# The first batch of a one-core attention and MLP kernel in a form of its own: doubled fp32r products, row sums by TensorE, bf16 transposes of W_tok, dummy products and another load order

## The chip, the core and the metric

The kernel runs on one core of a Trainium2 chip. The metric is the time of one execution on the device in microseconds (us); less is better. A profile is one such execution; its span is 1.8 to 2.1 us below the time of the same run. TensorE (PE) multiplies, ScalarE (ACT), VectorE (DVE) and GpSimd (POOL) do the rest, SyncE (SP) issues transfers. With one core there is no second die to compare with, so runs are labelled slow or fast by their times.

## The reference

Eight batches; per batch eight heads of 576 rows and 64 columns. Attention without softmax, an RMS norm over the 64 columns, then a token-mixing and a channel-mixing layer.

```python
kv  = einsum('bhsd,bhse->bhde', k, v)
out = einsum('bhsd,bhde->bhse', q, kv)
x   = out / sqrt(mean(out*out, -1) + 1e-6) * g_norm     # then to [b, 576, 512]
a1  = alpha1 * x + beta1
u   = x + lam * einsum('ts,bsd->btd', w_tok, a1)        # "tok"
a2  = alpha2 * u + beta2
y   = u + lam * (maximum(a2 @ w_ch1, 0) @ w_ch2)        # "ch1", "ch2"
```

The biases beta1 and beta2 are folded into spare rows, lam into W2 and the row sums of W_tok.

## The kernel before

The kernel describes each operation with its engine (or several to choose from), an assumed cost, what it reads and writes, and a priority. A list scheduler in the program, run when the kernel is built, turns this into one fixed order per engine. On the chip the orders are kept, with semaphores in between: an instruction that waits holds up what stands behind it on its engine (the stall of 3.30 us shown below is one).

Some terms. A main is the transfer of the first 512 rows of q, k or v of a batch (1 MB), a tail that of the last 64 (128 KB). A staging slot is a buffer in which a main or a block of weights lands. A cast or rounding copies it from there in the type that the products take; fp32r is the type of the rounded fp32 operands of kv, the q transposes and the attention output. An eviction copies the result of a product out of TensorE's accumulators. The result of a dummy product is not used.

```python
def load(b, pri):                      # batch 0: v on ScalarE's queue, the rest on SyncE's
    aq = "AQ" if b == 0 else "SP"
    load_main("k", k, b, "SP", pri)
    load_main("v", v, b, aq, pri)
    load_tail("k", kvft, k, b, 0, "SP", pri)       # rows 512 to 575
    load_tail("v", kvft, v, b, 64, aq, pri)
    load_main("q", q, b, "SP", pri)
    ...
# norm, per chunk of 128 rows
P.op({"ACT": act_us(512)}, ... ACT.Square ...)
P.op({"DVE": dve_us(512)}, ... tensor_reduce(out=small[rows, s4], in_=sq[rows, s2], ...) ...)
P.op({"ACT": 0.3}, ... ACT.Sqrt ...)
P.op({"DVE": 0.2}, ... reciprocal ...)
P.op({"DVE": dve_us(512)}, ... yn = product * scale ...)
...
# W_tok: 25 fp32 transposes, five evictions on ScalarE, then column sums by TensorE
P.op({"PE": 0.12}, lambda e, _, ...: e.transpose(t..., wrow(tc, sc), ident[0:rr, 0:rr]), ...)
```

Lines of the profile name products by what they write and read: `ps<-vr,kr` is kv, `ps<-identr,qr` the q transposes, `ps<-kvc,qt` or `ps<-kr,qt` the attention output, `ps<-rt,wt` tok, `ps<-a2t,w` ch1, `ps<-w,ht` ch2.

## Time and profile before

| kernel before | us |
|---|---|
| median of 3 runs (lowest, highest) | 385.44 (384.83, 387.29) |
| span of the profiled run (386.89 us) | 385.1 |
| first ch1 product starts | 52.49 |
| from there to the end of the last product | 327.31 |
| closing add and store | 5.31 |
| TensorE at half clock | 13.8 to 41.1, and by the pace of the dummies (one every 0.43 us) before 7.0, where no clock is recorded |

The start of the first ch1 product splits the kernel into the preparation of the first batch and TensorE's main work.

### The profile page before, as it was taken

Reading aid. Unit: us, or ns where it says so; the run is one execution under the profiler, and the core shown is the slowest. Engines: PE = TensorE matmul, PEld = TensorE weight load, DVE = VectorE, ACT = ScalarE, POOL = GpSimd, SP = SyncE. Lnnn points to the kernel's source line nnn. Section 1 sums busy time; section 2 is a strip of 40 time slices with the busy share of each in tenths; the row PEclk is TensorE's granted clock in tenths of the full one; section 3 lists DMA queues with packets and bytes.
Section 4 is the critical chain, followed back from the end, with each engine's and each line's share of the span. In section 5 each row is a group of like instructions: output and inputs, shape, how many; then the busy total and the mean of one; then the engine's idle time right before and its main releaser. Section 6 shows DMA issues by size and latency. Waiting matters only on the chain.

```text
span 385.1 us, 5526 instructions
## 1 busy us (share of the span) xinstructions
PE 371.8 (97%) x2243; PEld 228.4 (59%) x2243; DVE 224.6 (58%) x370; ACT 179.1 (47%) x309; POOL 81.2 (21%) x61
## 2 busy tenths in 40 slices
PE   5799999999999999999999999999999999999994
PEld 2496456557977656455875566456765544547641
DVE  6317689999696848665945398336815582520021
ACT  1346665756773727622662246423752165206400
POOL 2007242542034305101410034003400141000000
PEclk9755899999999999999999999999999999999998
DMA  8994799997994564402000111002000120010022
GB/s 236 305 380 146 210 384 327 303 277 238 329 306 140 155 203 136 139 2 83 29 0 2 54 56 28 0 29 75 9 2 27 54 56 0 25 59 27 2 82 54
DMA packets 47377, 47.83 MB, mean 124 GB/s; under 512 B 13869, under 2 KB 38453, under 8 KB 47224
## 3 DMA queue, kind: packets, MB, share of 16 engines
q1 hardware_dynamic: 45760, 46.29, 38.6%
q10 hardware_dynamic: 1592, 1.19, 1.1%
q8 instruction: 17, 0.28, 0.3%
q14 instruction: 8, 0.07, 0.1%
HBM read 38.04 MB, written 9.44 MB: 123 GB/s over the span
## 4 chain that ended last, share of the span: by engine, by line
PE 86%; DVE 8%; DMA 3%; issue 0%; ACTq 0%; ACT 0%
PE ps L700 30%; PE ps L720 30%; PE ps L634 11%; PE ps L595 3%; PE ps L539 3%; DMA st<-in_v_dram 3%; PE ps L557 3%; DVE w L904 2%; PE ps L661 2%; PE ps L849 2%; PE ps L788 1%; DVE qr L397 1%; DVE yn L610 1%; DVE small L602 1%; PE ps L867 1%; DVE vr L397 1%
## 5 line engine op out<-in xcount | busy, mean ns | idle before, releaser
L700 PE MATMUL ps<-a2t,w 128*128 128x320 bf16 (+1 forms) x768 | 141.7, 329 | 0.0
L720 PE MATMUL ps<-w,ht 128*128 128x512 bf16 x576 | 138.4, 382 | 0.0
L700 PEld LDWEIGHTS ps<-a2t,w 128*128 128x128 bf16 x768 | 73.5, 98 | 41.5
L685 ACT ACTIVATE ht<-ps 128x640 bf16<-128x640 f32 (+1 forms) x110 | 71.8, 653 | 51.2 <-PE ps L700 50.7
L720 PEld LDWEIGHTS ps<-w,ht 128*128 128x128 bf16 x576 | 54.6, 98 | 58.4
L620 POOL TENSOR_TENSOR xm<-yn,g_bc 128x512 f32<-128x512 f32 x22 | 37.0, 1680 | 167.4 <-DVE yn L610 166.7
L728 DVE TENSOR_TENSOR xm<-ps,xm 128x512 f32<-128x512 f32 x32 | 22.0, 689 | 57.7 <-PE ps L720 57.4
L600 ACT ACTIVATE sq<-ps 128x512 f32<-128x512 f32 (+1 forms) x40 | 23.7, 593 | 48.9 <-PE ps L595 48.6
L634 PE MATMUL ps<-rt,wt 128*128 128x512 bf16 x160 | 42.7, 381 | 0.0
L641 DVE TENSOR_TENSOR xm<-ps,xm 128x512 f32<-128x512 f32 x32 | 21.9, 689 | 34.9 <-PE ps L634 34.7
L539 PE MATMUL ps<-vr,kr 128*128 128x128 f32 x128 | 37.0, 387 | 2.0 <-DVE vr L397 1.9
L557 PE MATMUL ps<-identr,qr 128*128 128x128 f32 x128 | 37.0, 394 | 0.0
L595 PE MATMUL ps<-kvc,qt 128*128 128x128 f32 x128 | 36.5, 388 | 0.0
L602 DVE TENSOR_REDUCE small<-sq 128x8 f32<-128x512 f32 (+1 forms) x40 | 26.9, 677 | 16.0 <-ACT sq L600 15.6
L539 PEld LDWEIGHTS ps<-vr,kr 128*128 128x128 f32 x128 | 25.9, 217 | 3.5 <-DVE vr L397 3.0
L610 DVE TENSOR_TENSOR yn<-ps,small 128x512 f32<-128x512 f32 (+1 forms) x40 | 27.3, 685 | 0.6
L595 PEld LDWEIGHTS ps<-kvc,qt 128*128 128x128 f32 x128 | 25.9, 216 | 2.2 <-DVE qt L397 0.2
L615 POOL TENSOR_TENSOR rt<-yn,ge 128x512 bf16<-128x512 f32 x13 | 18.4, 1414 | 39.6 <-DVE yn L610 39.2
L557 PEld LDWEIGHTS ps<-identr,qr 128*128 128x128 f32 x128 | 26.1, 218 | 0.9 <-issue 0.3
L634 PEld LDWEIGHTS ps<-rt,wt 128*128 128x128 bf16 x160 | 15.4, 98 | 17.2 <-DVE xm L641 0.3
L396 ACT ACTIVATE qt<-ps 128x512 fp32r<-128x512 f32 x27 | 16.1, 597 | 16.1 <-PE ps L557 15.9
L788 PE MATMUL ps<-identb 128*128 128x512 bf16 x47 | 14.7, 454 | 4.2 <-DVE identb L771 4.2
(93 smaller groups left out, 346.8 us busy)
## 6 DMA issues: line engine op xcount, KB each, us to landing
st<-in_k_dram SPq DMA_DIRECT2D x8, 1024.0 KB, 8.5
st<-in_q_dram SPq DMA_DIRECT2D x8, 1024.0 KB, 7.3
st<-in_moe_w_ch_dram SPq DMA_DIRECT2D x8, 1024.0 KB, 11.7
out_dram<-xm SPq DMA_DIRECT2D x32, 256.0 KB, 2.3
st<-in_v_dram SPq DMA_DIRECT2D x7, 1024.0 KB, 6.3
ht<-in_moe_w_tok_dram SPq DMA_DIRECT2D x1, 1152.0 KB, 13.5
kvft<-in_k_dram SPq DMA_DIRECT2D x8, 128.0 KB, 4.8
qft<-in_q_dram SPq DMA_DIRECT2D x8, 128.0 KB, 7.5
```

The source lines that it names most:

```text
L539: return e.matmul(t.flat()[:, 128 * pr:128 * pr + 128], a, m, start=(c == 0), stop=(c == 4))
L557: return e.matmul(t.flat()[:, 128 * pr:128 * pr + 128], a, identr[:], start=True, stop=True)
L595: return e.matmul(t.flat()[:, 128 * pr:128 * pr + 128], a, kvc[:, b % 2, pr, :], start=True, stop=True)
L600: P.op({"ACT": act_us(512)}, lambda e, _: e.activation(flat(sq[rows, s2]), t.flat(rows), ACT.Square), r=[t], w=[("sq", s2)], pri=p)
L602: P.op({"DVE": dve_us(512)}, lambda e, _: e.tensor_reduce(out=small[rows, s4], in_=sq[rows, s2], axis=AX.X, op=ALU.add), r=[("sq", s2)], w ...
L610: P.op({"DVE": dve_us(512)}, lambda e, _: e.tensor_tensor(out=hview(yn[rows, s3, :]), in0=hview(t.flat(rows)), in1=small[rows, s4][:, :, N ...
L620: lambda e, _: e.tensor_tensor(out=hview(x), in0=hview(yn[rows, s3, :]), in1=g_bc[rows, None, :].to_broadcast([nr, NH, DH]), op=ALU.mult),
L634: return e.matmul(t.flat(), wt[:, sc, col:col + 128], rt[:, sc, :] if sc < 4 else rtt[:], start=(sc == 0), stop=(sc == 4))
L685: return e.activation(dst, src(), ACT.Relu)
L700: return e.matmul(o, w1[:, dj, 128 * fj:128 * fj + 128], m, start=(dj == 0), stop=(dj == 3))
L720: P.op({"PE": 0.216}, lambda e, _: e.matmul(t.flat(), ht[:, fj, 128 * c:128 * c + 128], w2[:, fj, :], start=(fj == 0), stop=(fj == 15)), r ...
L728: P.op({"DVE": dve_us(512)}, lambda e, _: e.tensor_tensor(out=x, in0=t.flat(), in1=x, op=ALU.add), r=[t] + keys, w=keys, pri=p - 2)
```

## The change

Its intent is to shorten those 52 us: q, k, v load first; the products that cannot be wide are doubled to 256 columns so that TensorE counts as busy; dummy products fill TensorE's idle time from 1 us on; the sums of squares of batch 0 go to TensorE (transposed products, squared, multiplied by a block of ones); W_tok is transposed in bf16; a sixth staging slot lets loads run further ahead. The cost table of the scheduler changes too, so every order in the kernel is new. Core of the diff, cuts marked:

```diff
-        st = sb("st", [128, 5, 2048], F32)
+        st = sb("st", [128, NS, 2048], F32)                  # NS = 6
+        hot = sb("hot", [128, 128], BF16)                    # operand of the dummies
+        blk = sb("blk", [128, 2], F32)                       # ones, per head
...
             aq = "AQ" if b == 0 else "SP"
+            load_main("q", q, b, "SP", pri)
             load_main("k", k, b, "SP", pri)
-            load_main("v", v, b, aq, pri)
-            load_tail("k", kvft, k, b, 0, "SP", pri)
+            load_main("v", v, b, "SP", pri, 2 if b == 0 else 1)
+            if b == 0:
+                load_tail("q", qft, q, 0, 0, aq, pri)
+            load_tail("k", kvft, k, b, 0, aq, pri)
             load_tail("v", kvft, v, b, 64, aq, pri)
...
+        def norm_first(pri):
+            def sums(pr, c):
+                P.op({"PE": 0.1}, lambda e, _: e.matmul(
+                    ts.flat()[:, 8 * c + 2 * pr:8 * c + 2 * pr + 2],
+                    sqt[:, pr, 128 * c:128 * c + 128], blk[:], start=True, stop=True), ...)
+            for pr in range(4):
+                ... # transposed product of 512 columns, Square on ScalarE into sqt (fp32)
+                for c in range(4):
+                    sums(pr, c)
+            ... # the last 64 rows likewise; one Sqrt and one reciprocal for all
...
+            for i in range(2):
+                P.op({"POOL": pool_us(1152, False)}, ...)     # W_tok to bf16 on GpSimd
...
-                P.op({"ACT": act_us(512)} if qn < 2 else {"ACT": ..., "DVE": ...}, ...)   # W1
+                P.op({"ACT": act_us(512)} if qn < 3 else {"ACT": ..., "DVE": ...}, ...)
-                P.op({"POOL": pool_us(1024), "DVE": dve_us(1024)}, ...)                   # W2
+                P.op({"POOL": pool_us(1024)} if hh else {"DVE": dve_us(1024)}, ...)
-        norm(0, -400)
+        norm_first(-400)
```

## The prediction

> **What bounds the kernel now.** I read the page's tenths, then the windows table, the chain that ended last in order of time, the groups by line, and last the matmul-by-matmul timeline of TensorE and the DMA issues. The page first:
>
> ```profile
> span 385.1 us, 5526 instructions
> ...
> PE   5799999999999999999999999999999999999994
> ...
> PEclk9755899999999999999999999999999999999998
> DMA  8994799997994564402000111002000120010022
> ```
>
> TensorE looks full everywhere, but its granted clock is low in the first five slices (48 us), and DMA pauses in slice 5. The windows table (columns: stretch and its length, then busy time of PE, PEld, DVE, ACT, POOL with counts, granted clock, DMA share, GB/s) separates the start:
>
> ```profile
> 0.00:13.60 13.60, 9.44 (x30) 3.53 (x30) 6.63 (x17) 3.51 (x7) 1.96 (x9) 1.00 0.91 260
> 13.60:15.50 1.90, 0.00 (x1) 0.00 (x0) 1.23 (x1) 1.55 (x3) 0.00 (x0) 0.56 1.26 243
> 15.50:41.00 25.50, 24.72 (x97) 18.97 (x97) 12.26 (x26) 11.84 (x24) 8.20 (x6) 0.50 0.71 247
> 41.00:52.50 11.50, 11.42 (x69) 5.61 (x69) 9.32 (x16) 7.75 (x14) 1.42 (x2) 0.99 1.02 316
> ```
>
> After 1.9 us in which TensorE had nothing to do, the whole first batch, 15.5 to 41 us, ran at half clock. The chain shows what the time was spent on (start, us, what):
>
> ```profile
> 2.97 11.26 DMA st<-in_v_dram
> 14.26 1.24 DVE vr L397
> ...
> 17.96 3.31 PE ps L539 x16
> ...
> 22.57 3.52 PE ps L557 x17
> ...
> 27.37 3.63 PE ps L595 x17
> 31.00 1.22 PE ps L849 x5
> ...
> 32.94 5.41 PE ps L849 x20
> 38.35 1.82 PE ps L867 x4
> ```
>
> It waits for v, rounds it, and then goes in single file through kv, the q transposes, the q·kv products (all fp32r with 128 columns), the fp32 transposes of W_tok (L849) and its column sums; tok follows at 44 us and the first ch1 matmul (L700) starts at 52.5 us, in the timeline. From there I compared start-to-start times: 216 ns for a bf16 matmul of 512 columns, 136 for 320, 56 for a transpose, and 74 for an fp32r matmul between bf16 ones (251 + 39 - 216). Summing the matmuls at these prices from 52.5 us to the last one at 379.8 gives 324 us of 327.3, so only 3.2 us are lost after the start, nearly all before 130 us. The last 5.3 us are the closing add and store. So the steady part is TensorE's work itself, and the change can win only in the first 52.5 us.
>
> **What the Trainium skill says.** "TensorE: Matmul & The Clock Gate", § What's actually happening: the array has half its clock until a free-running window of 3413 ns was busy, and loses it after an idle one. The trace agrees on the window: its clock changes come at 7.0, 13.8 and 41.1 us, and 41.1 - 13.8 is 8 x 3.41. It records no clock before 7.0, but dummies from 4.16 us start every 0.43 us, twice the 0.216 of later ones. It adds something: fp32r matmuls that keep TensorE "busy" for 20 us did not bring the clock back; the 512-column sums (L867) did. Same page, § LDWEIGHTS: columns / 1.2 ns, 107 ns for 128. The trace's back-to-back fp32r pairs start 213 ns apart at half clock (107 of load + 107 of streaming) and about 161 at full (107 + 54), so such loads are not hidden behind each other. "DMA: Bandwidth & Descriptors", § Issuing engines are not separate DMA queues: queues share the same 16 engines. It agrees: v, issued at 2.97 us on ScalarE's queue, landed at 14.2 after sharing with q, which landed at 13.2. "SBUF — State Buffer", § Who interferes with whom: VectorE copies in two-port mode and operations on two SBUF inputs block against GpSimd for a whole instruction. It agrees: the 128x512 cast of q takes 427 ns, but 2584 ns beside GpSimd's 128x1024 multiply.
>
> **The change, part by part.** I place the first ch1 matmul anew.
>
> Loads. Before, 1 MB each of k, q, v and the 64-row tails were in at 13 to 16 us, W_tok at 20.4, W1 at 22.8, 25.6, 28.3 and 32.1 (2.7 us per MB). The new order q, k, v with tails on the other queue carries 3.1 MB + 0.4 MB before W_tok. The bytes counted over time in the old trace pass 3.55 MB at about 13.5 us; so q lands near 6.5, k near 10, v (in two halves) near 12 and 13.5, W_tok near 18, W1 by 29. v itself gains under 1 us. But q's rounding and transposes (4 casts, 20 matmuls, 5 evictions of 0.6 us) now fit ahead of v.
>
> Products. After v: two casts side by side (0.42 on VectorE, 0.62 on ScalarE), 14.3 us; second half of kv, 10 matmuls of 256 columns at 0.117 (the kernel's assumption) to 0.214 (107 + 107), 16.2; small evictions, 16.9. Duplicating the columns costs streaming time; its point is that the array counts as busy, with the dummies, which now start near 1 us instead of 4.2. If the clock holds, dummies and products run at full rate.
>
> Norm. Before, each of five chunks had a square, reduce (0.68), sqrt (0.30), reciprocal (0.19) and multiply (0.69) in turn. Now ScalarE squares a transposed product for 5 x 0.6 us, two of them before v's second half, TensorE sums by 20 tiny fp32 matmuls (two 0.1 us loads each, some 0.25 us with streaming, 1 us of it after the last square), one sqrt, one reciprocal: scales ready near 21 us. Then VectorE makes five x (0.69) and three rt (0.69) while GpSimd makes two rt (1.41 each): 5.5 us, 26.5; with W_tok's evictions on the same engine and some blocking by GpSimd, 28.5.
>
> W_tok. GpSimd casts 2880 columns; at 0.74 us per 512, 4.2 us after 18, i.e. 22. 25 bf16 transposes at 0.056 to 0.11 us replace 25 fp32 ones that took 6.6 us; five evictions on two engines, 2 us; sums 1.3; two vector steps 0.65 + 0.82: 27. So it ends beside the norm chain, not after it.
>
> Tok and on. Four of five products per chunk can run ahead. After the last operand (28.5): one matmul, four adds of 0.69 in turn, a cast 0.63, transposes, a scaled eviction 0.77: 4.6 us, 33. In-order queues filled from an assumed timetable, not from events, usually cost some; I add 2.5 us. The first ch1 starts near 35.5 instead of 52.5: **17 us**.
>
> After it. TensorE's work is unchanged (four more fp32r matmuls for batch 1's own tail, 0.3 us). But batch 1 and W2 now come later relative to ch1: q1, k1, v1 follow W1 at about 32, 35 and 38 us, W2 at 41 to 49, scaled near 53, while the first ch2 (18 us after ch1 in the old trace: 71.0 - 52.5) wants it from 54. The sixth slot matters here: before, v of batch 1 sat 18 us behind a ScalarE cast that had to free its slot. VectorE was busy 41 of 44 us between 52 and 96 and takes on 2.5 us of rounding that used to precede ch1. I expect 4 us lost in place of 3.2. Sum: 385.4 - 17 + 0.3 + 0.8 = **369.5 us**.
>
> **Rivals.** (1) The gain shrinks to 8 to 10 us, 376: VectorE/GpSimd blocking or W2's scaling (2.4 us a half on GpSimd, 1.1 to 2.9 on VectorE) becomes the new limit after ch1. For it: VectorE's 95% there and a DMA that then must run without pause to about 60 us. Against it: TensorE has 5 us of batch 1's fp32r work to fill in with, and 20 MB, all that is needed through batch 2, is in by 60 us at 0.36 MB/us. (2) The clock stays low in spite of dummies because TensorE stands before an operand that comes late, and dummies behind it cannot run: the first batch's products and tok would then take about twice as long, some 4 us more, 373. For it: one gap of 1.9 us cost the clock for 27 us before. (3) Everything fits as the new timetable assumes: ch1 near 32.5, 366. Slower than before would need the stall after ch1 to grow by 17 us; I see nothing of that size.
>
> **Range and chances.** Start of ch1 between 31 and 41, losses after it of 2 to 8 us: 363 to 377. Over 2% faster means under 377.7; that needs 8 of the 17 us. Faster 0.94, within 2% 0.05, slower 0.01.
>
> **What would show it.** Right: first ch1 at 33 to 39 us, clock full from about 7 us through the first batch, bf16 transposes of W_tok under 3 us in all, DMA without the pause of slice 5, the same 216/136/74 ns after it and the same 5 us of tail. Wrong: half clock again between 15 and 40; VectorE instructions of 2 us and more while GpSimd casts W_tok; TensorE gaps between 40 and 80 us that end with W2 or a rounding of batch 1; or a different pace after 130 us, which I take as untouched.

## The result

The changed kernel took 397.32 us (median of 4 runs, 395.19 to 399.92), beside 385.66 for the kernel before (4 runs). The ratio is 1.03, 95% interval 1.0225 to 1.0375: about 3% slower. Ratios here are the mean time of one kernel's fast runs over the mean of the other's of the same rounds, so not quite the ratio of the medians quoted.

The page of the changed kernel (tenths in 40 slices of 9.9 us):

```profile
span 394.5 us, 5549 instructions
...
PE   8789988999979999899999999999999999999994
...
PEclk9865699999999999999999999999999999999999
DMA  8996599999864921821100011002000210020021
```

TensorE is busier in the first two slices than before, then the clock is low in slices 3 to 5. New dips of PE stand in slices 12 and 17, long after the start. Measured as before: ch1 begins at 56.73 us (before 52.49), from there to the last product 332.36 (before 327.31), tail 5.36. So of the 9.4 us that the span grew, 4.2 came before ch1 and 5.1 after it. (The medians differ by 11.7 us. The profiled run of the kernel before was a slow one, 386.89 us, and that of the changed kernel was below its median, 396.33.) The windows table of the changed kernel (stretch and length, then busy time of PE, PEld, DVE, ACT, POOL with counts, granted clock, DMA share, GB/s):

```profile
14.00:22.04 8.04, 4.74 (x23) 2.92 (x21) 2.15 (x6) 0.76 (x2) 4.30 (x4) 0.92 1.03 323
22.04:27.10 5.06, 5.06 (x12) 2.58 (x10) 1.80 (x6) 2.88 (x9) 0.00 (x0) 0.50 1.05 387
27.10:38.60 11.50, 11.50 (x57) 11.38 (x56) 1.39 (x2) 1.63 (x3) 0.00 (x0) 0.50 0.77 255
38.60:45.90 7.30, 7.05 (x37) 4.14 (x37) 4.16 (x7) 4.32 (x8) 2.55 (x2) 0.50 0.19 46
```

TensorE was idle for 3.3 of the 8.04 us of the first stretch. Then the clock was half for 24 us (22.0 to 45.9; it had been half from 11.8 to 15.2 as well), and for 11.5 of these (third row) TensorE was full while the three other engines did almost nothing. The transfers paused too: their share falls to 0.77 and 0.19, while SyncE's next load waited 16.1 us for ScalarE's rounding of W1 to free a staging slot. TensorE's timeline names the pieces (start, us, engine, line, product, count, and in brackets the idle time before it and what ended it):

```profile
21.45 0.76 PE L598 MATMUL ps<-vrt,krt 128*128 128x256 f32 x4 [3.30 <-DVE vrt L400]
...
27.13 1.87 PE L717 MATMUL ps<-blk,w 128*128 128x2 f32 x8
28.86 0.45 PE L732 MATMUL ps<-qtt,kvc 128*128 128x128 f32 x1
29.11 1.81 PE L717 MATMUL ps<-blk,w 128*128 128x2 f32 x8
```

Two things stand out. The stall of 3.30 us ends with the rounding of v's tail, vrt. And each eight of the sum products with the ones block take about 1.8 us; 40 of them are recorded where the program has 20, so each fp32 sum runs as two, some 0.21 us each at half clock. Lastly the tails among the DMA issues (KB, us from issue to landing):

```profile
qft<-in_q_dram ACTq DMA_DIRECT2D x1, 128.0 KB, 8.7
kvft<-in_k_dram ACTq DMA_DIRECT2D x1, 128.0 KB, 10.5
kvft<-in_v_dram ACTq DMA_DIRECT2D x1, 128.0 KB, 16.0
```

v's tail of 128 KB, issued at 4.66 us, landed at 20.69, after both parts of W_tok (18.71 and 19.38), which were issued later. The trace says how. Its packets by queue (1 is SyncE's, 10 ScalarE's), counted from its records:

```
window us   queue 1                          queue 10
14 to 16    82 packets, 722 KB (9216 B)      81 packets,  21 KB (256 B)
16 to 18   149 packets, 450 KB (2 to 9 KB)  148 packets,  37 KB (256 B)
```

The sizes in brackets are those of the packets that carry nearly all bytes. In these windows the two queues send packet for packet (from 10 to 14 us as well, 813 against 806), so the queue with 256-byte packets got a thirty-fifth of the other's bytes in the first window (21 against 722 KB) and a twelfth in the second. After 18 us the tail had fewer packets left than the other queue sent (88 against 173 up to 19.4 us).

### The profile page after: what moved, and what is told of

The parts are those of the page before. It is cut to its first block, busy times and chain, and to the rows that moved or that the text cites. A ratio compares the mean times of both kernels' runs of the same rounds, so it can differ in the third digit from the quotient of the medians.

```text
span 394.5 us, 5549 instructions
## 1 busy us (share of the span) xinstructions
PE 375.2 (95%) x2240; PEld 232.9 (59%) x2271; DVE 231.4 (59%) x383; ACT 173.8 (44%) x300; POOL 81.4 (21%) x61
## 3 DMA queue, kind: packets, MB, share of 16 engines
q1 hardware_dynamic: 45760, 47.08, 38.5%
## 4 chain that ended last, share of the span: by engine, by line
PE 84%; DVE 9%; DMA 4%; issue 1%; ACTq 1%; ACT 1%
PE ps L858 32%; PE ps L838 29%; PE ps L771 10%; DMA kvft<-in_v_dram 4%; PE ps L584 4%; PE ps L598 2%; PE ps L717 2%; PE ps L799 2%; DVE vr L400 1%; DVE yn L698 1%; DVE ht L824 1%; PE ps L996 1%; DVE small L686 1%; DVE kr L400 1%; PE ps L580 1%
## 5 line engine op out<-in xcount | busy, mean ns | idle before, releaser
L823 ACT ACTIVATE ht<-ps 128x512 bf16<-128x512 f32 (+1 forms) x111 | 72.0, 649 | 52.5 <-PE ps L838 52.0
L704 POOL TENSOR_TENSOR xm<-yn,g_bc 128x512 f32<-128x512 f32 x28 | 45.0, 1607 | 184.7 <-DVE yn L698 184.2
L684 ACT ACTIVATE sq<-ps 128x512 f32<-128x512 f32 (+1 forms) x35 | 20.7, 592 | 47.7 <-PE ps L584 47.4
L598 PE MATMUL ps<-vr,kr 128*128 128x128 f32 (+1 forms) x128 | 35.8, 373 | 2.9 <-DVE vr L400 2.9
L808 ACT ACTIVATE a2t<-ps,cols 128x512 bf16<-128x512 bf16 (+1 forms) x16 | 12.4, 826 | 47.6 <-PE ps L799 47.6
L584 PE MATMUL ps<-kvc,qt 128*128 128x128 f32 x112 | 33.0, 387 | 0.0
L584 PE MATMUL ps<-identr,qr 128*128 128x128 f32 x112 | 29.6, 362 | 0.0
L701 DVE TENSOR_TENSOR rt<-yn,ge 128x512 bf16<-128x512 f32 x28 | 26.7, 955 | 0.4
L771 PEld LDWEIGHTS ps<-rt,wt 128*128 128x128 bf16 x160 | 15.5, 98 | 17.6
L698 DVE TENSOR_TENSOR yn<-ps,small 128x512 f32<-128x512 f32 (+1 forms) x35 | 24.0, 685 | 0.5
L584 PEld LDWEIGHTS ps<-kvc,qt 128*128 128x128 f32 x112 | 22.3, 199 | 2.3
L584 PEld LDWEIGHTS ps<-identr,qr 128*128 128x128 f32 x112 | 21.2, 200 | 0.6
L399 ACT ACTIVATE qt<-ps 128x512 fp32r<-128x512 f32 x25 | 14.8, 595 | 7.0 <-PE ps L584 6.9
```

The costliest lines, as they stand in the source:

```text
L584: return e.matmul(t.flat()[:, 128 * pr:128 * pr + 128], a(), m(), start=start, stop=stop)
L598: return e.matmul(t.flat()[:, at:at + w], a, m, start=(c == 0), stop=(c == 4))
L698: P.op({"DVE": dve_us(512)}, lambda e, _: e.tensor_tensor(out=yn[rows, s3, :].rearrange("p (r h d) -> p r h d", r=4, h=2), in0=heads(t, b, ...
L701: P.op({"DVE": dve_us(512), "POOL": pool_us(512)}, lambda e, _: e.tensor_tensor(out=rto, in0=yn[rows, s3, :], in1=ge1[rows, :], op=ALU.mul ...
L704: P.op({"POOL": pool_us(512)}, lambda e, _: e.tensor_tensor(out=hview(x), in0=hview(yn[rows, s3, :]), in1=g_bc[rows, None, :].to_broadcast ...
L771: return e.matmul(t.flat(), wt[:, sc, col:col + 128], rt[:, sc, :] if sc < 4 else rtt[:], start=(sc == 0), stop=(sc == 4))
```

## The experiments

All kernels gave correct results. The first theory is that two faults add up: the late tail (stall, and with it the clock) and the fp32 sums. Its rivals are that either is enough, that the clock goes anyway, or that the new order as such is bad. In the second series one of seven runs of the kernel before took 758.73 us; it is not among the fast runs.

### Tails on SyncE's queue, orders otherwise the same (e1)

```diff
-        P.schedule()
+        P.schedule(); [setattr(o, "eng", "SP") for o in P.ops if o.kind == "L" and o.eng == "AQ"]
```

> The same program on every compute engine; only the three 64-row tails of batch 0 go out on SyncE's queue after v instead of on ScalarE's. Theory (late tail): v's tail lands by about 17 us instead of 20.7, the 3.3 us stall of TensorE before the vrt products goes under 0.5 us, the clock is not lost at 22.0 us, and the first ch1 matmul comes 8 to 12 us earlier than 56.7; time about 388. Rival (the small fp32 sums lose the clock by themselves): the stall goes, but the clock still falls in one of the next windows (25 to 29 us), the first ch1 comes 3 to 5 us earlier; time about 393.

Measured: 389.63 us median of four runs, 383.5 to 391.52. Three were labelled slow and one fast (383.5, mean granted clock 0.983 against 0.966 to 0.971), which here means that the clock was low for a shorter time, so I give no ratio. The profiled run is one of the slow ones (389.59). In it v's tail landed at 14.8 and the stall was gone; ch1 began at 48.34. But the clock fell all the same at 20.0 us and stayed at half until 37.1 (a line of TensorE's timeline, then one of the windows table):

```profile
16.03 0.74 PE L598 MATMUL ps<-vrt,krt 128*128 128x256 f32 x4 [0.29 <-DVE vrt L400]
...
20.00:37.10 17.10, 16.86 (x83) 14.00 (x83) 5.13 (x9) 5.95 (x11) 3.75 (x4) 0.50 0.95 321
```

The late tail explains the stall and, in this profile, 8.4 us of the start of ch1; the clock needs more than its absence.

### bf16 squares and ones, tails still late (e2)

```diff
-        blk = sb("blk", [128, 2], F32)
+        blk = sb("blk", [128, 2], BF16)
-        sqt = w2f[:, 0:2560].rearrange(...)
+        sqt = w2[:].rearrange("p j c -> p (j c)")[:, 0:2560].rearrange(...)
```

> The same order on every engine; squares and the block of ones are bf16, so each of the 20 sums is one matmul instead of two. Theory (sums mis-sized): the 40 sum matmuls take 8.4 us of TensorE in the current kernel; 20 at 0.11 us take 2.2, so the first ch1 comes about 6 us earlier even with the late tail; time about 391. If the sums lie beside other waits (W_tok's casts, ScalarE): under 2 us, 396.

Measured: 390.1 us (389.22 to 390.33), ratio 1.011 (1.0083 to 1.0137); ch1 at 48.96. TensorE's timeline of this run:

```profile
21.28 1.23 PE L598 MATMUL ps<-vrt,krt 128*128 128x256 f32 x4 [4.37 <-DVE vrt L400]
...
27.43 0.26 PE L717 MATMUL ps<-blk,w 128*128 128x2 bf16 x4
27.56 0.45 PE L732 MATMUL ps<-qtt,kvc 128*128 128x128 f32 x1
```

The stall is still there and longer, but each sum is one product now, and four of them let the next product start 0.13 us after the first. In all they lie between 27.4 and 31.4 in place of 27.1 and 38.5, also at half clock. So the sums, too, are worth 7 us by themselves.

### Both repairs (e3)

> Tails on SyncE's queue and bf16 sums together. If late tail and sums are the two causes, the clock stays full through the first batch and ch1 starts at 38 to 42 us, time 378 to 383, under before. If the clock is lost for another reason, ch1 at 46 to 50 and about 388.

Measured: 379.17 us (378.04 to 379.76), ratio 0.9827 (0.9799 to 0.9856). That is 18.1 us less than the changed kernel and better than the kernel before. TensorE's page row, clock row and timeline:

```profile
PE   8898999999799998999999999999999999999994
...
PEclk9999699999999999999999999999999999999999
```

```profile
16.05 0.74 PE L598 MATMUL ps<-vrt,krt 128*128 128x256 f32 x4 [0.38 <-DVE vrt L400]
...
19.46 0.25 PE L717 MATMUL ps<-blk,w 128*128 128x2 bf16 x4
19.58 0.31 PE L732 MATMUL ps<-qtt,kvc 128*128 128x128 f32 x1
...
20.51 1.17 PE L580 MATMUL ps<-kr,qt 128*128 128x256 f32 x8
...
27.60 4.49 PE L771 MATMUL ps<-rt,wt 128*128 128x512 bf16 x20
31.93 1.24 PE L771 MATMUL ps<-rtt,wt 128*128 128x512 bf16 x5
...
34.62 1.27 PE L584 MATMUL ps<-identr,qr 128*128 128x128 f32 x7 [1.24 <-DVE qr L400]
```

The clock was full from 4.2 to 38.4 us and ch1 began at 40.76. In the profiles ch1 moves from 56.7 to 48 or 49 with one repair and to 40.8 with both: about 8 us each, and together their sum. The clock is lost for one period of 6.8 us at 38.4.

### Filling the stall with more dummies (e4)

The tail stays late; the four dummies ahead of the vrt products are issued five times each.

```diff
-                ins = o.fn(eng, o.eng)
+                ins = [o.fn(eng, o.eng) for _ in range(self.times.get(o, 1))][-1]
... # self.times is 5 for those four dummies
```

> The late tail stays; the four dummies ahead of the vrt products are issued 20 times (4.3 us), so that TensorE is busy during the stall. Theory (the stall costs by the clock, not by its 3.3 us): the clock is not lost at 22.0 us; if the sums hold it, ch1 comes 6 to 10 us earlier, about 389. If the sums cannot hold it, it falls some 3.4 to 6.8 us later and ch1 comes under 3 us earlier, about 395.

Measured: 394.55 us (393.82 to 394.75), ratio 1.0226 (1.0199 to 1.0253). Its timeline:

```profile
16.16 4.49 PE L931 MATMUL ps<-hot 128*128 128x512 bf16 x20
20.93 0.74 PE L598 MATMUL ps<-vrt,krt 128*128 128x256 f32 x4 [0.28 <-DVE vrt L400]
...
24.34 1.48 PE L717 MATMUL ps<-blk,w 128*128 128x2 f32 x8
```

The stall is filled and the clock is kept past it, to 24.8 us; then it falls until 41.8. The fp32 sums had begun only 0.4 us before; the work of the window ahead of the fall is that of e1's (see the clock, below). ch1 began at 53.27, 3.5 us earlier, and the time fell by 2.8 us. So a filled stall alone is worth little: the clock was only saved to be lost 2.7 us later than in the changed kernel.

### GpSimd's halves of the W2 scaling given to VectorE (e5)

This looks at the 5.1 us after ch1. In the changed kernel GpSimd scales four halves of W2 between 56.4 and 66.8 us, and VectorE's two roundings of v (batch 1) at that time are slow. The rows are count and duration in ns (least, median, most), then first and last start, of the changed kernel:

```profile
L400 DVE CAST vr<-st x2: 2681/2758/2834, 56.6 to 59.2; 128x1024 fp32r<-128x1024 f32 x2
```

```profile
L1048 POOL TENSOR_TENSOR w<-st,lam_bc x4: 2346/2548/2692, 56.4 to 64.4; 128x1024 bf16<-128x1024 f32 x4
```

```diff
-        P.schedule()
+        P.schedule(); [setattr(o, "eng", "DVE") for o in P.ops if o.tag[:3] == "w2." and o.eng == "POOL"]
```

> The changed kernel with one thing moved: the four halves of W2 that GpSimd scales are given to VectorE, at the same place of the order; nothing else differs. Theory (GpSimd's 2.5 us multiplies block VectorE's two casts of batch 1's v, which take 5.4 us in place of 1.3, and TensorE waits 2.9 us for them after the first ch1): the two casts take 0.7 each, the waits of TensorE between 57 and 63 us fall from 2.9 to under 0.7 us; VectorE gains 4 x 1.1 us of work, which may give up to 2 us back later; time 393 to 396. Rival (v is late by its DMA): the waits stay, time 398 or more.

Measured: 393.06 us (389.96 to 394.78), ratio 1.0188 (1.0129 to 1.0247). The same row in this run:

```profile
L400 DVE CAST vr<-st x2: 673/674/674, 58.4 to 59.0; 128x1024 fp32r<-128x1024 f32 x2
```

The same roundings took a quarter of the time, TensorE's wait of 2.9 us for them was gone, and the part after ch1 fell from 332.36 to 329.17. In this profile ch1 began 1.5 us later (58.28; half clock from 12.5 to 50.0), so its span shows less of the gain (1.7 us) than the medians do (4.3).

### The norm as before, tails repaired (e6)

```diff
-            aq = "AQ" if b == 0 else "SP"
+            aq = "SP"
-        norm_first(-400)
+        norm(0, -400)
```

> Tails on SyncE's queue, and the first batch's norm per chunk as before (square, reduce, sqrt, reciprocal, multiply), without the sums by TensorE; everything is put in order anew. If the sums by TensorE are what made the first batch slow once the tails are in time, this is close to the kernel with bf16 sums or better: ch1 at 40 to 44 us, time 378 to 384. If the transposed sums are in principle better and only their fp32 form is wrong, this is 3 to 6 us slower than the bf16 sums: 382 to 386.

Measured: 389.45 us (385.68 to 391.27), ratio 1.0091 (1.0014 to 1.0167); ch1 at 47.99, with the clock lost three times before 53 us. That is outside both expected ranges. The edit goes in before the timetable is made, so the order changes too. Beside e3 (379.17) the kernel with row sums by TensorE in bf16 is some 10 us faster. How much of that is the norm and how much the new order and its clock was not separated. Nor does it say what the fp32 form gained: e1's runs lie on both sides of this one.

### A timetable made for later landings (e7)

Both repairs put in before the scheduler runs, a sum counted as 0.06 us, and transfers assumed to land 0.5 to 2 us later.

```diff
-                        o.end = dma_free + 2.0
+                        o.end = dma_free + (2.5 if dma_free < 15 else 4.0)
```

> Tails on SyncE's queue and bf16 sums, and the timetable that orders the instructions is told later landings (2.5 us after the transfer for the first loads, 4.0 for later ones, in place of 2.0) and 0.06 us per sum; everything is put in order anew. Theory (VectorE stands 1.9 us in order before the cast of batch 1's q, with the five adds of tok behind it, because the timetable has that load 2 us early): that idle time goes, the clock is not lost at 38 us, ch1 starts at 37 to 39 us in place of 40.8; time 374 to 377. Rival (such waits merely move): within 1.5 us of 379.

Measured: 381.66 us (380.95 to 382.15), ratio 0.99 (0.9875 to 0.9924). ch1 came earlier than in e3 (39.84), but the part after it was 335.14, with waits at new places. It lost 4 us there and gained 1 ahead, and lies outside both expected ranges.

### Both repairs, no dummies (e8)

> The kernel with tails on SyncE's queue and bf16 sums, its dummies dropped and nothing else changed. If the dummies make the clock of the first batch: half clock until about 25 us or later, ch1 3 to 8 us later than 40.8, time 382 to 387. If the products of 256 columns do it by themselves: the clock is full from about 10 us, time within 1.5 us of 379.

Measured: 380.26 us (378.63 to 380.55), ratio 0.9851 (0.9815 to 0.9886). ch1 at 43.79. The clock has no record before 28.8 us, so the page's row is no witness; the timeline is. The eight products that take 1.17 us in e3 take 2.02 here:

```profile
25.71 2.02 PE L580 MATMUL ps<-kr,qt 128*128 128x256 f32 x8
```

The dummies bring ch1 forward by 3 us, but e8 then keeps full clock where e3 loses it for 6.8 us, so 1 us is left.

### Both repairs, and W2's halves on VectorE (e9)

> The kernel of both repairs (tails on SyncE, bf16 sums; 379.2 us, 331.0 us from the first product of ch1 on), with GpSimd's four halves of the W2 scaling given to VectorE as well. Theory: they hold up VectorE's two vr casts and so TensorE by about 3 us after ch1, as in the late-tail kernel (there 393.1 against 397.3): the casts fall to about 1.3 us for the two, the part after ch1 to 328, the whole to 376.5 (374.5 to 378). Rival: with the first batch early the GpSimd work lies elsewhere in time, TensorE waits for something else there, and the time stays at 379 (378 to 380.5).

Measured: 378.34 us (377.9 to 379.11), ratio 0.9805 (0.9777 to 0.9832). It falls just outside the theory's range and inside the rival's. In e3 the vr roundings of batch 1 already took 0.69 us each: they ran from 41.6 to 42.9 us, before GpSimd's work on W2 began at 46.7. So the collision of e5 is itself a result of the late start. In this profile half clock ended at 42.1 in place of 45.2, which is enough for the 1.1 us that the part after ch1 gained.

### W1's roundings free between ScalarE and VectorE (e10)

Both repairs before the scheduler runs, a sum counted as 0.06 us, and:

```diff
-                P.op({"ACT": act_us(512)} if qn < 3 else {"ACT": act_us(512), "DVE": dve_us(512, 2)}, ...
+                P.op({"ACT": act_us(512)} if qn < 0 else {"ACT": act_us(512), "DVE": dve_us(512, 2)}, ...
```

> Both repairs put in before the timetable is made, a sum counted as 0.06 us, and one thing freed: ScalarE no longer has to make every rounding of W1, VectorE may take any of them. Theory: the 2.4 us that TensorE idles some 55 us after ch1 began, and the stalls of 1.0 and 1.6 us near it, are in the timetable itself (its own plan shows 2.2 and 1.1 us there, and none with this freed: 368.3 planned against 364.0), since ScalarE is over-full there: the stall of 1.6 us goes below 0.6, the part after ch1 to 327 to 329, the whole to 376 (373 to 378.5). Rival: the stall comes from what the plan has no idea of (VectorE blocked by GpSimd, transfers landing late), and a new timetable only moves it: 379 to 383, as with the later-landings timetable (381.7).

Measured: 376.94 us (376.54 to 377.83), ratio 0.9769 (0.9741 to 0.9797): the fastest here, and faster than the kernel before by over 2%. TensorE's two largest waits from 38 to 165 us (in total, times, longest), e3 first:

```profile
PE ps L838 <- ACT ht L823: 2.4, 3, 1.6
PE ps L838 <- DVE ht L824: 1.0, 1, 1.0
```

```profile
PE ps L598 <- DVE vr L400: 3.2, 3, 1.7
PE ps L838 <- ACT ht L823: 0.5, 1, 0.5
```

The waits on ScalarE's ht, the evictions of ch1's result, fell from 2.4 to 0.5 us, as the theory said. But 3.2 us of waits for v's roundings came in their place, and the part after ch1 stayed at 331.24 where the theory had 327 to 329. In the profile the gain is all in the earlier ch1 (39.15 against 40.76), not in the term I named.

### Five slots (e11), and all of it free (e12)

Both with the repairs before the scheduler runs. e11 changes `NS = 6` to 5. e12 has that, W1 free, W_tok's casts free among three engines, and tok of batch 0 in the order of chunks.

> Both repairs before the timetable is made, a sum counted as 0.06 us, and five staging slots in place of six. Theory: the sixth slot is worth nothing here, since no idle time of TensorE after ch1 is a wait for a staging transfer; the plan itself is 1.8 us shorter with five (366.5 against 368.3): 379 (376.5 to 381). Rival: with five slots the weights of the next stage land later and TensorE waits for them: over 382.

> Both repairs before the timetable is made, a sum counted as 0.06 us, five slots, W1's roundings free between ScalarE and VectorE, the W_tok casts free among three engines, and the first batch's token products in the order of their chunks, so that four of the five of each chunk need W_tok only and not the norm. The plan has no stall of TensorE near ch1 of the second batch (365.1). Theory: as with W1 freed, 376 (373 to 378.5); the token products no earlier than the W_tok chain lets them be, ch1 still at 39 to 41. Rival: the new timetable only moves the stalls: 379 to 383.

Measured: e11 379.36 us (378.84 to 380.81), ratio 0.9834 (0.9796 to 0.9872), the same as e3. Nothing here shows a gain from the sixth slot, though no kernel with six slots and otherwise the same inputs was run. e12 377.52 us (376.79 to 378.02), ratio 0.978 (0.9753 to 0.9807), ch1 at 40.99. The freed casts and the other tok order did not bring ch1 forward.

## Why the prediction was wrong

It said 369.5 us and the time was 397.32. It failed ahead of ch1, on two terms, and to a smaller part after it.

**Loads.** Most mains were right: q landed at 6.3 us (said 6.5), k at 10.0 (10), v's first half at 12.3 (12), W_tok's main part at 18.7 (18). v's second half came at 14.7 (13.5), after the 14.2 of the kernel before, so v gained nothing; with the tails on SyncE's queue (e1) it came at 12.6. The step that failed is "The new order q, k, v with tails on the other queue carries 3.1 MB + 0.4 MB before W_tok". I counted bytes as if both queues were one line. They alternate by packet, so the last tail came at 20.69, behind W_tok's 9216-byte packets. I had cited one section of the Trainium skill's "DMA: Bandwidth & Descriptors" and missed another: § Queues, rings and completion order says that an engine goes round the queues that have work at packet granularity. The trace before shows no such lag: v's tail landed at 15.9. There W_tok was issued later (6.2 us against 5.0) and v's main part shared ScalarE's queue; which of the two mattered was not tested. e1 shows the stall go when the tails move; ch1 comes 8.4 us earlier.

**Products and clock.** "If the clock holds" was the right condition. Rival (2) named the mechanism (TensorE stands before a late operand, and the dummies behind cannot run), and the trace shows it: TensorE was busy for 0.6 of the 3.4 us before 22.04, and the clock fell there. Its size, 4 us, was too small: half clock then lay over the sums as well, for 23.9 us in all. The reading that stood for it, that one gap of 1.9 us cost the clock in the kernel before, does not fit that trace: the clock fell at 13.8 us, when the gap (13.6 to 15.5) had just begun. What came before the fall is under "Clock" below. Two small readings were off as well: k was in at 6.5 us before, not at 13 to 16, and pairs of fp32r products at full clock start 163 to 166 ns apart in the three places where the trace has them, not 161.

**Norm.** "20 tiny fp32 matmuls (two 0.1 us loads each, some 0.25 us with streaming, 1 us of it after the last square)" is the second term that failed. It made 5 us of TensorE, 1 of them on the path. They were 40 products of about 0.21 us, some 8.4 us, all on the path, between 27.1 and 38.5, with the W_tok transposes behind them in order. The reciprocal started at 39.6 in place of 21. I had priced them as if they lay beside the squares, but ScalarE had finished the four wide squares at 26.0, and TensorE was the one engine at work. e2 shows 7.2 us for these alone, e3 18.1 for both. With both repaired the reciprocal started at 22.7: the step was right in its mechanism for bf16.

**W_tok and tok.** With both repairs ch1 still began at 40.8, not 35.5. The step is "Four of five products per chunk can run ahead". In e3 none ran before W_tok's chain was done: the 25 tok products lie in one row from 27.6 to 33.0, where I had one product after the last operand. The adds then waited behind VectorE's rounding of batch 1's q, whose transfer landed at 33.85. e12, with an order meant to let them run ahead, began tok even later (30.9). The timetable itself has this. Run by itself, the scheduler in the kernel plans ch1 at 39.9 us before the change and at 38.6 after it, a gain of 1.3 us. The two plans use different cost tables, though: with three prices of the changed kernel (an fp32r product alone, a pair of them, GpSimd's operations) the old program plans ch1 at 43.8, so on one scale the plan gains about 5 us, still far from 17. The chip missed the first plan by 12.6 us and the second by 18.1; e3 missed it by 2.2. e3 thus gains mostly by running as planned.

**After ch1.** I allowed 0.3 + 0.8 us and got 5.1. Rival (1), blocking by GpSimd, was there: 3.2 us in e5. Against it I had argued that batch 1's fp32r work would fill in, but that work itself waited for the blocked roundings. In e3 and e9 the collision does not arise, as ch1 comes earlier. Some 3.4 us of waits in ch1 stay (2.4 on ScalarE and 1.0 on VectorE); they are partly in the timetable, and e10 shows that removing one sort raises another. That the part after ch1 does not return to 327.3 in any variant is measured; no experiment pinned it to one cause.

**Clock.** In e10 the clock fell at 20.3 us, after a window in which TensorE was never idle (windows table: the full-clock window, then the next):

```profile
16.89:20.30 3.41, 3.41 (x23) 2.05 (x21) 2.28 (x7) 2.90 (x9) 1.59 (x2) 1.00 1.02 273
20.30:23.70 3.40, 3.40 (x23) 3.21 (x23) 1.70 (x4) 1.75 (x3) 1.45 (x2) 0.50 1.06 390
```

The work in it is v's tail products, 64-row transposes, four wide products, two one-row broadcasts and the first sums. e1 lost it in the same work (window 16.6 to 20.0), also at 100% busy, and so did e4 (21.4 to 24.8), e7, e11 and e12 (falls at 21.1, 20.9 and 22.0 us), while e3, whose window edges fall at 17.85 and 21.27, did not. So busy time is not what decides, and the fp32 sums are not needed for a fall.

A count on the same traces, made afterwards and tested by no experiment, comes close. It gives each product 0.216 us per 512 streamed columns, the measured pace at full clock, times the share of the 128 rows that it uses, and adds this up over each window of 3.41 us at full clock, up to 90 us or more, in the 13 traces that record a fall. All 19 falls come after windows with a share of at most 0.37. Of the 344 windows after which the clock stayed, 340 have more, and four have 0.33 to 0.36. In e10's window the two one-row broadcasts take 1.06 us of busy time and add next to nothing; its share is 0.32. e3's window at the same work has 0.38, so it kept the clock by little. The window before the fall at 13.8 us in the kernel before has 0.30. The count doesn't tell when the clock comes back. A fall here would account for e1's spread of 8 us; I did not trace its other runs.

## What to carry to other kernels

Before moving a small transfer to another queue, ask how large its packets are and what stands beside it in the other queue: with 256-byte packets against 9216-byte ones it finishes last, however early it was issued. Price tiny products from a trace at the clock and type they will have (fp32 was two products each), and count them on TensorE's own line when nothing runs beside them. And when an order is planned from assumed costs, read first what the plan itself promises: here 1.3 us ahead of ch1 (about 5 on one cost table), against the 17 I derived from single steps. And where the clock matters, don't take busy time for activity: here one-row products filled a window and the clock fell after it.

## What the Trainium skill lacked or had wrong

- "TensorE: Matmul & The Clock Gate" gives full clock after a busy window and half after an idle one. In e10 the clock fell after a window of 3.41 us that the profile shows 100% busy, and in the changed kernel TensorE was busy 23.6 of the 23.9 us at half clock. Of what counts as activity the page says only that transposes in TensorE's transpose mode do not in the same way, and e10's window has none of those (its 64-row transposes are ordinary products with an identity). A share of streamed columns times rows below about 0.37 goes with the falls of these traces (19 of 19).
- "DMA: Bandwidth & Descriptors" has the packet-wise round robin cited above, and this case agrees (82 packets against 81, 149 against 148). It does not draw the consequence where it advises on queues: a 128 KB load of 256-byte packets landed 16.0 us after its issue beside a load of 9216-byte ones, and on the other queue (e1) at 14.8 us in place of 20.7.
- No page gives a time for a tiny fp32 product ("FP8 and Floating Point Precision" only counts the passes of true fp32, four): with two columns it ran as two products of about 0.21 us each at half clock, where four bf16 ones (e2) held the next product up by only 0.13 us at half clock.
